# A decode kernel that streams its caches: VectorE's program as a loop over head groups, queries projected as rows, 24 instead of 16 blocks of V turned at the end

## The chip, the cores and the metric

One core of a Trainium2 chip. The metric is the device time of one execution in microseconds (us); lower is better. All runs told here were in the undisturbed ("fast") state. The profile is one execution taken by the hardware profiler; its span is about 1.8 us shorter than the time that the same execution reports.

Names: PE is TensorE, DVE is VectorE, ACT is ScalarE, POOL is GpSimd, SP is SyncE, which issues the big DMAs here. The profile counts 16 DMA engines, and each large transfer has 16 completion events in the trace, taken as one per engine. The *lag* is the time from the first of these 16 events of a transfer to the last; where no transfer is named, it is the last piece of V.

## The reference, cut

```python
# A: one decode step of attention.  Hq=16, Hkv=8, Sk=65536, Dh=256, D=448, all bf16
q = (x @ wq).reshape(1, 1, 16, 256)          # two query heads share one K/V head
p = softmax(q @ k.T / 16)                    # k, v: 8 x 65536 x 256 each
a = (p @ v).reshape(1, 1, 4096) @ wo
# B: layernorm(x), an outer product with w1 and b1, gelu, a sum with w2 and b2: 448 numbers
g = sigmoid((x * gate_w).sum(-1))
out = g * a + (1 - g) * b                    # 448 numbers
```

K and V are 268 MB each. Each byte is used once, so the kernel is a stream of 544 MB from HBM with little work on each piece.

## The kernel before

Each of the eight K/V heads (a "group") is cut into six chunks of 6, 6, 5, 5, 5, 5 steps, a step being 16 blocks of 128 rows; 48 chunks in all. A chunk of K is 6 or 5 MB (6144 or 5120 KB in the profile) and goes into one of two buffers; a chunk of V goes into a third. Per chunk VectorE turns K (5 or 6 transposes of 2.28 us), PE computes scores, ScalarE exponentiates, VectorE turns the probabilities, PE multiplies with V one chunk later, VectorE adds the result to `og`. PE's program is already a hardware loop; VectorE's is written out, all 48 chunks of it.

```python
        def load_k(i):
            n = steps[i] * SB * DH
            if i >= 2:
                sp.wait_ge(s_s, cum[i - 1])            # scores of chunk i-2 done
            sp.dma_start(out=kbuf[i % 2][:, 0:n], in_=kv_src(A_k_cache, i)).then_inc(s_k[i % 2], 16)

        def load_v(i):
            n = steps[i] * SB * DH
            if i >= 1:
                sp.wait_ge(s_pv, i)                    # PV of chunk i-1 done
            sp.dma_start(out=vbuf[:, 0:n], in_=kv_src(A_v_cache, i)).then_inc(s_v, 16)
        # ... (cut)
        def project(e):                                # queries as columns: 128 matmuls of one column
            for c in range(2):
                for h in range(HQ):
                    dst = q_ps[:, c * HQ + h:c * HQ + h + 1]
                    for k in range(KA):
                        e.matmul(dst, lhsT=wqa_v[:, k, h, :, c], rhs=xT[:, k:k + 1],
                                 start=(k == 0), stop=False)
                    # ... one more for the last 64 rows of wq (cut)
        # ... (cut)
        for i in range(total):                         # VectorE, straight-line code
            g, c = divmod(i, PER)
            turns(i)
            if 0 < i < total - 1:
                dve.wait_ge(s_pv, i)
                drain_pv((i - 1) % PER == 0)           # two instructions, 256 columns each
                # ... at a group's end: denominators, s_g (cut)
            # ... turn the probabilities, next queries (cut)
```

The last chunk of V arrives in four pieces, of 48, 16, 12 and 4 blocks. The first 64 blocks are used "upright" (probabilities as weights, V as the moving side, then a drain by VectorE and a turn of the result on PE, the "o-turn"). The last 16 are used "turned": V itself is the weights, two matmuls of two columns a block, and they need no drain.

```python
        edges = [0, (steps[-1] - 2) * SB, (steps[-1] - 1) * SB, steps[-1] * SB - TAIL, steps[-1] * SB]
        # ... (cut)
        pe.wait_ge(s_last[0], 16)
        for s in range(steps[-1] - 2):
            p_v(vlast, pT_t[1], s, False, False)
        # ... (cut)
        pe.wait_ge(s_last[1], 16)
        p_v(vlast, pT_t[1], steps[-1] - 2, False, True).then_inc(pe_sem, 1)
        dve.wait_ge(pe_sem, 3)
        drain_pv(False)
        # ... (cut)
        o_turn(2)
        for j in range(SB):
            if j in (0, SB - TAIL):
                pe.wait_ge(s_last[2 if j == 0 else 3], 16)
            # ... two turned matmuls per block (cut)
```

The softmax here doesn't subtract the row's maximum and nothing guards it: scores larger than these inputs give would overflow.

Of the kernel before, what the change touches and what calls it, by code (L numbers as in the profile page):

```python
# [14 lines left out]
HQ = 16  # L15
HKV = 8
# [13 lines left out]

TAIL = 4
# [4 lines left out]
PE = mybir.EngineType.PE  # L36

# [55 lines left out]
def kernel(  # L93
# [55 lines left out]
    one_b = const.tile([1, 128], BF16, name="one_b")  # L149
# [24 lines left out]
    den = [const.tile([128, PER], FP32, name=f"den{i}") for i in range(2)]  # L174
# [3 lines left out]
    og = const.tile([128, DH], FP32, name="og")  # L178
# [8 lines left out]
    M0, M1, R0, R1, D0, D1, DA_, DB_ = range(8)  # L187
    offsets = {
        M0: [(0, 2)], M1: [(2, 4)], R0: [(0, 1), (2, 3)], R1: [(1, 2), (3, 4)],
# [14 lines left out]
    def critical():  # L204
# [9 lines left out]
        s_pv = nc.alloc_semaphore("s_pv")  # L214
        s_g = nc.alloc_semaphore("s_g")
# [15 lines left out]
        def load_k(i):  # L231
            n = steps[i] * SB * DH
            if i >= 2:
                sp.wait_ge(s_s, cum[i - 1])
            sp.dma_start(out=kbuf[i % 2][:, 0:n], in_=kv_src(A_k_cache, i)).then_inc(s_k[i % 2], 16)

        def load_v(i):
            n = steps[i] * SB * DH
            if i >= 1:
                sp.wait_ge(s_pv, i)  # L240
            sp.dma_start(out=vbuf[:, 0:n], in_=kv_src(A_v_cache, i)).then_inc(s_v, 16)
# [34 lines left out]
        for t, key, val in (  # L276
            (one_b, "one_b", 1.0), (xd, "xd", 0.0), (one_f, "one_f", 1.0), (zero_b, "zero_b", 0.0),
            (pat, "pat", 0.0), (qw, "qw", 0.0), (col_f, "col_f", 1.0), (pv, "pv", 0.0),
        ):
            do("dve", lambda e: e.memset(t[:], val), writes=[key])  # L280
# [11 lines left out]
        def turn_x(e):  # L292
            for k in range(KA + 2):
                if k < KA:
                    src = x_row[:, 0:DA].rearrange("o (p k) -> o p k", k=KA)[:, :, k]
                else:
                    src = xd[:, k - KA, :]
                last = e.matmul(
                    x_ps[:, k:k + 1], lhsT=src, rhs=one_b[:, 0:1], start=(k == 0),
# [25 lines left out]
        for col, sign in ((0, -1.0), (1, 1.0)):  # L325
# [25 lines left out]
            "pe", lambda e: e.matmul(xb_ps, lhsT=one_b[:], rhs=x_row[:], start=True, stop=True),  # L351
# [75 lines left out]
        q_ps = misc[:, 448:448 + 2 * HQ]  # L427
        wqa_v = wqa.rearrange("p k (h d two) -> p k h d two", h=HQ, two=2)
        wqb_v = wqb.rearrange("p (h d two) -> p h d two", h=8, two=2)

        def project(e):
            for c in range(2):
                for h in range(HQ):
                    dst = q_ps[:, c * HQ + h:c * HQ + h + 1]
                    for k in range(KA):
                        e.matmul(
                            dst, lhsT=wqa_v[:, k, h, :, c], rhs=xT[:, k:k + 1],
                            start=(k == 0), stop=False,
                        )
                    x_h = KA + h // 8  # L440
                    last = e.matmul(
                        dst, lhsT=wqb_v[:, h % 8, :, c], rhs=xT[:, x_h:x_h + 1],
                        start=False, stop=True,
                    )
            return last

        do("pe", project, reads=["wqa", "wqb", "xT", "x_ps"], writes=["q_ps", "x_ps"])
        do.need("sp", writes=["wqa", "wqb"])
        load_v(0)
        load_wo(0)  # L450
# [23 lines left out]
        def queries(g, r):  # L474
            h = 2 * g + r
            cols = slice(PAD + 16 * r, PAD + 16 * r + 97, 32)
            return dve.tensor_tensor(
                out=qw[:, :, cols], in0=qr[:, :, h:h + 1].to_broadcast([128, 8, 4]),
# [4 lines left out]
        for r in range(2):  # L483
            do("dve", lambda e: queries(0, r), reads=["qr", "block"], writes=["qw"])
# [7 lines left out]
        for i in range(total - 1):  # L492
            if i + 2 < total:
                load_k(i + 2)
            if i + 1 < total - 1:
                load_v(i + 1)
            if i % PER == 0 and i > 0:
                load_wo(i // PER)
# [3 lines left out]
        sp.wait_ge(s_s, cum[total - 1])  # L502
        edges = [0, (steps[-1] - 2) * SB, (steps[-1] - 1) * SB, steps[-1] * SB - TAIL, steps[-1] * SB]
# [7 lines left out]
        user = [0, 0, 0]  # L511
# [3 lines left out]

        def turns(i):
            kn = kbuf[i % 2][:].bitcast(FP32)
            dve.wait_ge(s_k[i % 2], 16 * (i // 2 + 1))
            for t, (s, b) in enumerate(blocks(i)):
                ins = dve.transpose(  # L520
                    out=kT[b][:].bitcast(FP32), in_=kn[:, s * SB * 128:(s + 1) * SB * 128]
                )
                if user[b]:
                    ins._wait_ge(s_s, user[b])
                ins.then_inc(s_kt, 1)
                user[b] = cum[i] + t + 1

        s_d = nc.alloc_semaphore("s_d")
        done = [0]

        def chain(ins, wait=True):
            if wait and done[0]:
                ins._wait_ge(s_d, done[0])
            done[0] += 1
            ins.then_inc(s_d, 1)

        def drain_pv(first):
            if first:
                chain(dve.tensor_scalar(  # L539
                    out=og[:], in0=pv[:, 0:DH], scalar1=mask[:, M0, 0:1], scalar2=None, op0=ALU.mult  # L540
                ))
            else:
                chain(dve.scalar_tensor_tensor(  # L543
                    out=og[:], in0=pv[:, 0:DH], scalar=mask[:, M0, 0:1], in1=og[:],
                    op0=ALU.mult, op1=ALU.add,
                ))
            chain(dve.scalar_tensor_tensor(  # L547
                out=og[:], in0=pv[:, DH:2 * DH], scalar=mask[:, M1, 0:1], in1=og[:],
                op0=ALU.mult, op1=ALU.add,
            ))  # L550

        def den_rows(g):
            chain(dve.tensor_tensor(out=dmul[:], in0=den[g % 2][:], in1=dmask, op=ALU.mult))
            chain(dve.tensor_reduce(out=dsum[:], in_=dmul[:], axis=AXIS.X, op=ALU.add))

        o_ps = misc[:, 504:512].rearrange("p (c v) -> p c v", v=4)
        do.need("dve", reads=["mask", "bias", "hw2", "h_bc", "qr", "w1T", "b1T"])
        do.need("dve", reads=["block"])
        for i in range(total):
            g, c = divmod(i, PER)  # L560
            turns(i)
            if 0 < i < total - 1:
                dve.wait_ge(s_pv, i)
                drain_pv((i - 1) % PER == 0)
                if c == 0:
                    den_rows(g - 1)
                    ins = dve.tensor_scalar(
                        out=og[:], in0=og[:], scalar1=dsum[:, 0:1], scalar2=None, op0=ALU.add
                    )
                    ins._wait_ge(s_d, done[0])  # L570
                    ins.then_inc(s_g, 1)
            pT = pT_t[1 if i == total - 1 else 0]
            ins = dve.transpose(out=pT[:], in_=p_t[:])  # L573
            ins._wait_ge(s_e, i + 1)
            ins.then_inc(s_pt, 1)
            if c == PER - 1 and g + 1 < HKV:
                for r in range(2):
                    queries(g + 1, r)
            if c == 0 and i > 0:
                dve.wait_ge(s_wo, 16 * g)  # L580
                dve.wait_ge(s_o, g)
                chain(dve.reciprocal(out=rden[:], in_=o_ps[:, 0, 2:4]))
                chain(dve.tensor_scalar(
                    out=rden[:], in0=rden[:], scalar1=gate[:, 0:1], scalar2=None, op0=ALU.mult
                ))
                ins = dve.tensor_tensor(
                    out=oT[:].rearrange("p (c r) -> p c r", r=2), in0=o_ps[:, :, 0:2],
                    in1=rden[:].rearrange("p (o r) -> p o r", o=1).to_broadcast([128, 2, 2]),
                    op=ALU.mult,
                )  # L590
                ins._wait_ge(s_d, done[0])
                ins.then_inc(s_ot, 1)
# [4 lines left out]
        for i in range(total):  # L597
            g, c = divmod(i, PER)
            ins = act.activation(  # L599
                out=p_t[:], in_=sc[:], func=ACT.Exp, scale=scale, accum_out=den[g % 2][:, c:c + 1]  # L600
            )
            ins._wait_ge(s_s, cum[i + 1])
# [44 lines left out]
        def scores(s, b, first, last):  # L647
# [8 lines left out]
            ins.then_inc(s_s, 1)  # L656

        def p_v(vt, pT, s, first, last):
            pT = pT[:].rearrange("p (i b x) -> p i b x", b=4, x=16)
            for k in range(SB // 2):  # L660
# [5 lines left out]
                    stop=last and k >= SB // 2 - 4, tile_position=(0, 32 * a), skip_group_check=True,  # L666
# [3 lines left out]
        def o_turn(width):  # L670
            for cc in range(2):
                ins = pe.matmul(  # L672
                    o_ps[:, cc, 0:width], lhsT=og[:, cc::2],
                    rhs=mask[:, R0:R0 + width, 0], start=(cc == 0), stop=(cc == 1),
                    skip_group_check=True,
                )
# [46 lines left out]
        fin = Order.__new__(Order)  # L723
        fin.__dict__.update(do.__dict__)
        for t, (s, b) in enumerate(blocks(last_i)):
            scores(s, b, t == 0, t == steps[-1] - 1)
        pe.wait_ge(s_pt, 1).then_inc(s_pt, -1)
        pe.wait_ge(s_v, 16).then_inc(s_v, -16)
        for s in range(steps[-2]):
            p_v(vbuf, pT_t[0], s, s == 0, False)  # L730
        dlast = (HKV - 1) % 2
        dve_sem = nc.alloc_semaphore("s_fd")
        pe_sem = nc.alloc_semaphore("s_fp")

        den_rows(HKV - 1)
        dve.wait_ge(s_d, done[0])
        dve.nop().then_inc(dve_sem, 1)
        pe.wait_ge(dve_sem, 1)
# [3 lines left out]
        ).then_inc(pe_sem, 1)  # L742
        pe.wait_ge(s_mp, turn)
        pe.matmul(
            acc[0:1, 0:D], lhsT=col_f[:], rhs=ymix[:], start=False, stop=True, skip_group_check=True,
        ).then_inc(pe_sem, 1)
        ins = dve.reciprocal(out=rden[:], in_=den_ps[:, 0:2])
        ins._wait_ge(pe_sem, 1)
        chain(ins, False)
# [97 lines left out]
```

## Time and profile before

| | before |
|---|---|
| time, median (range) of 3 runs | 1269.69 us (1269.68 to 1269.99) |
| span of the profiled run | 1268.7 us |
| data queue, share of 16 engines | 99.3% |
| last V piece: first and last engine to complete | 1258.60 and 1262.89 us |
| from there to the end | 5.8 us |

First, lines of the page of before: span, busy time by engine, and the DMA queues (packets, MB, share of 16 engines' span).

```profile
span 1268.7 us, 10632 instructions
PE 713.1 (56%) x4364; PEld 278.3 (22%) x4364; DVE 673.9 (53%) x511; ACT 50.1 (4%) x127; POOL 76.7 (6%) x98
q1 hardware_dynamic: 16728, 544.22, 99.3%
q8 instruction: 4, 0.07, 0.0%
q14 instruction: 9, 0.07, 0.0%
```

No compute engine is near full and the data queue is: the kernel is bound by the stream. The two "instruction" queues look like nothing, 0.14 MB of 544.

Next, four windows of 1 us near the end of before: length, busy time (and instructions) of PE, PE's weight loads, DVE, ACT and POOL, then the granted TensorE clock, the DMA share, and GB/s.

```profile
1258.00:1259.00 1.00, 0.95 (x12) 0.39 (x16) 0.00 (x0) 0.00 (x0) 0.00 (x0) 0.52 0.70 279
1259.00:1260.00 1.00, 1.00 (x16) 0.28 (x9) 0.00 (x0) 0.00 (x0) 0.00 (x0) 0.50 0.22 86
1260.00:1261.00 1.00, 1.00 (x16) 0.10 (x8) 0.00 (x0) 0.00 (x0) 0.00 (x0) 0.50 0.08 33
1261.00:1262.00 1.00, 0.90 (x16) 0.11 (x8) 0.00 (x0) 0.00 (x0) 0.00 (x0) 0.77 0.06 27
```

The stream does not stop at once. It trickles out at 33 and 27 GB/s, which is what one engine of 16 moves (434/16 = 27). One engine is late. The 16 completion events of the last piece of before, sorted and counted from the first:

```
first engine 1258.60; then +0.01 +0.04 +0.11 +0.29 +0.33 +0.40 +0.50 +0.51 +0.52 +0.53 +1.05 +1.48 +1.54 +2.01 +4.29
largest lag over time:  2.1 to 2.4 (28 to 617 us), 2.8 (from 623), 3.6 (from 910), 4.4 (from 1186)
8192-byte instruction packets at 49, 322, 332, 381, 617, 850, 905, 1184 us; 16384-byte ones at 19, 26, 1255, 1264 us
```

The events do not say which engine they belong to, so "the late engine" is read from how the sorted lags step up, just after a packet. The last two steps, from 2.62 to 3.57 us at 905 and from 3.46 to 4.44 at 1184, are 0.95 and 0.98; between packets the lag shrinks again a little. Up to 617 us the largest lag is that of another engine, late since the packets of 16384 bytes, so the packets at 49 and 332 do not show in it.

The packets carry no engine's name either, but a count gives it: from 49 to 332, 617, 905 and 1184 us the trace records 123, 130, 132 and 129 instructions of VectorE (its waits included), about as many each time (128.5 on average). So these packets are taken as the fetches of VectorE's code, and the code that one of them brings is called a fetch block below.

Last, the tail of before in order of time (start, duration, engine, line, operation, output<-inputs, count, idle time before and what ended it).

```profile
1258.05 2.73 PE L663 MATMUL pv<-kbuf,pT 128*4 128x512 bf16 x24 [2.09 <-DMA kbuf<-in_A_v_cache_dram]
1261.19 0.72 PE L663 MATMUL pv<-kbuf,pT 128*4 128x512 bf16 x8
1262.03 0.48 DVE L543 SCALAR_TENSOR_TENSOR og<-pv,mask,og 128x256 f32<-128x256 f32 x1 [5.36 <-PE pv L663]
1262.55 0.48 DVE L547 SCALAR_TENSOR_TENSOR og<-pv,mask,og 128x256 f32<-128x256 f32 x1
1263.15 0.63 PE L672 MATMUL misc<-mask,og 128*128 128x2 f32 x4 [1.24 <-DVEq L773]
1263.64 0.97 PE L783 MATMUL misc<-pT,kbuf 128*128 128x2 bf16 x32
1264.64 0.16 DVE L789 TENSOR_TENSOR oT<-misc,rden 128x4 bf16<-128x4 f32 x1 [1.61 <-PE misc L783]
1265.76 0.67 SPq L810 DMA_DIRECT2D out_dram<-res  x1
```

The last data is there at 1262.89, but the o-turn (L672) starts only at 1263.15 and the turned matmuls (L783) stand behind it. They end 1.7 us after the last data. A PE at a granted clock of 0.5 is called cold below.

### The profile page before, as it was taken

How to read it: one execution, taken by the hardware profiler on the slowest of the kernel's cores; microseconds unless marked ns; L12 is line 12 of the kernel's file. 1: busy time of each engine (PE TensorE's matmuls, PEld its weight loads, DVE VectorE, ACT ScalarE, POOL GpSimd, SP SyncE). 2: the span in 40 equal slices, each digit the busy share in tenths (PEclk: the TensorE clock that was granted, in tenths of full speed). 3: DMA queues.
4: the chain of work that ended last, by engine and by line, in shares of the span. 5: the costliest groups of instructions: out<-in, count | busy, mean ns of one | idle time of the engine just before them, and what ended most of it. 6: DMA issues, size and time to landing. Idle time of an engine off the chain costs nothing. (4 is left out here: it accounts for less than half of the span.)

```text
span 1268.7 us, 10632 instructions
## 1 busy us (share of the span) xinstructions
PE 713.1 (56%) x4364; PEld 278.3 (22%) x4364; DVE 673.9 (53%) x511; ACT 50.1 (4%) x127; POOL 76.7 (6%) x98
## 2 busy tenths in 40 slices
PE   2845656466444655566556664565545655466546
PEld 1312222122211222222122221222212221122212
DVE  4745555465545645555456554565446644465444
ACT  0000000000000000000000000000000000000000
POOL 0001010110110101101101011000000000000000
PEclk9887877768877787778877787778777888778777
DMA  9999999999999999999999999999999999999996
GB/s 412 420 441 434 425 435 437 431 434 438 439 426 427 434 435 433 438 428 434 440 436 429 430 434 432 434 438 434 434 427 444 427 430 434 436 430 429 436 433 294
DMA packets 16831, 544.36 MB, mean 429 GB/s; under 512 B 1841, under 2 KB 3891, under 8 KB 4275
## 3 DMA queue, kind: packets, MB, share of 16 engines
q1 hardware_dynamic: 16728, 544.22, 99.3%
q8 instruction: 4, 0.07, 0.0%
q14 instruction: 9, 0.07, 0.0%
q10 hardware_dynamic: 90, 0.01, 0.0%
HBM read 544.22 MB, written 0.00 MB: 429 GB/s over the span
## 5 line engine op out<-in xcount | busy, mean ns | idle before, releaser
L652 PE MATMUL sc<-kT,qw 128*128 128x512 bf16 x2048 | 565.0, 438 | 463.9 <-PEq L648 463.9
L520 DVE STREAM_TRANSPOSE kT<-kbuf 128x2048 f32<-128x2048 f32 x256 | 571.2, 2283 | 328.1 <-DMA kbuf<-in_A_k_cache_dram 292.2
L652 PEld LDWEIGHTS sc<-kT,qw 128*128 128x128 bf16 x2048 | 213.8, 108 | 813.5 <-issue 649.6
L663 PE MATMUL pv<-vbuf,pT 128*4 128x512 bf16 x2008 | 129.2, 409 | 57.2 <-PEq L694 56.8
L573 DVE STREAM_TRANSPOSE pT<-p_t 128x512 bf16<-128x512 bf16 x48 | 34.1, 711 | 95.0 <-ACT p_t L599 95.0
L543 DVE SCALAR_TENSOR_TENSOR og<-pv,mask,og 128x256 f32<-128x256 f32 x39 | 18.9, 483 | 115.3 <-PE pv L663 115.3
L663 PEld LDWEIGHTS pv<-vbuf,pT 128*4 128x4 bf16 x2008 | 50.5, 91 | 133.9 <-issue 93.9
L599 ACT ACTIVATE p_t<-sc 128x512 bf16<-128x512 f32 x48 | 28.7, 597 | 1192.7 <-PE sc L652 1192.7
L626 POOL TENSOR_SCALAR t_b<-t_b 128x448 f32<-128x448 f32 x14 | 7.9, 564 | 358.5 <-ACT t_b L608 358.5
L630 POOL TENSOR_SCALAR t_b<-t_b,hw 128x448 f32<-128x448 f32 x14 | 9.2, 660 | 335.6 <-ACT t_b L616 335.6
L547 DVE SCALAR_TENSOR_TENSOR og<-pv,mask,og 128x256 f32<-128x256 f32 x47 | 22.7, 484 | 1.7
L539 DVE TENSOR_SCALAR og<-pv,mask 128x256 f32<-128x256 f32 x8 | 3.9, 484 | 36.7 <-PE pv L663 36.7
L629 POOL TENSOR_TENSOR t_b<-t_b,u_b 128x448 f32<-128x448 f32 x14 | 15.8, 1127 | 1.2
L634 POOL TENSOR_TENSOR t_b<-t_b,u_b 128x448 f32<-128x448 f32 x14 | 15.8, 1126 | 1.2
L635 POOL TENSOR_TENSOR ymix<-ymix,t_b 128x448 f32<-128x448 f32 x14 | 15.8, 1126 | 1.1
L716 PE MATMUL acc<-wo,oT 128*1 128x448 bf16 x28 | 7.4, 391 | 13.7 <-PEq L713 13.7
L608 ACT ACTIVATE t_b<-h_bc,b1T,w1T 128x448 f32<-128x448 f32 x14 | 10.5, 748 | 0.0
L622 POOL TENSOR_SCALAR u_b<-h_bc,w1T,b1T 128x448 f32<-128x448 f32 x14 | 10.0, 714 | 4.1 <-DVE pat L419 2.7
L599 ACT ACTIVATION_READ_ACCUMULATOR p_t<-sc 128x1 f32 x48 | 9.3, 194 | 0.0
L616 ACT ACTIVATE t_b<-t_b 128x448 f32<-128x448 f32 x14 | 7.9, 566 | 0.0
L672 PEld LDWEIGHTS misc<-mask,og 128*128 128x128 f32 x32 | 4.9, 195 | 2.9 <-DVEq L773 1.9
L716 PEld LDWEIGHTS acc<-wo,oT 128*1 128x1 bf16 x28 | 2.0, 84 | 15.9 <-issue 14.6
(88 smaller groups left out, 60.5 us busy)
## 6 DMA issues: line engine op xcount, KB each, us to landing
kbuf<-in_A_k_cache_dram SPq DMA_DIRECT2D x32, 5120.0 KB, 32.0
vbuf<-in_A_v_cache_dram SPq DMA_DIRECT2D x31, 5120.0 KB, 21.7
kbuf<-in_A_k_cache_dram SPq DMA_DIRECT2D x16, 6144.0 KB, 35.8
vbuf<-in_A_v_cache_dram SPq DMA_DIRECT2D x16, 6144.0 KB, 25.4
wo<-in_A_wo_dram SPq DMA_DIRECT2D x8, 448.0 KB, 23.8
vbuf<-in_A_wq_dram SPq DMA_DIRECT2D x1, 3072.0 KB, 10.0
kbuf<-in_A_v_cache_dram SPq DMA_DIRECT2D x1, 3072.0 KB, 27.1
kbuf<-in_A_v_cache_dram SPq DMA_DIRECT2D x1, 1024.0 KB, 29.1
```

Source lines behind the costliest of these rows:

```text
L520: ins = dve.transpose(out=kT[b][:].bitcast(FP32), in_=kn[:, s * SB * 128:(s + 1) * SB * 128])
L543: chain(dve.scalar_tensor_tensor(out=og[:], in0=pv[:, 0:DH], scalar=mask[:, M0, 0:1], in1=og[:], op0=ALU.mult, op1=ALU.add,))
L547: chain(dve.scalar_tensor_tensor(out=og[:], in0=pv[:, DH:2 * DH], scalar=mask[:, M1, 0:1], in1=og[:], op0=ALU.mult, op1=ALU.add,))
L573: ins = dve.transpose(out=pT[:], in_=p_t[:])
L599: ins = act.activation(out=p_t[:], in_=sc[:], func=ACT.Exp, scale=scale, accum_out=den[g % 2][:, c:c + 1])
L608: ins = act.activation(out=t_b[:], in_=h_bc[:], func=ACT.Square, scale=w1T[:, b:b + 1], bias=b1T[:, b:b + 1],)
L622: lambda: pool.tensor_scalar(out=u_b[:], in0=h_bc[:], scalar1=w1T[:, b:b + 1], scalar2=b1T[:, b:b + 1], op0=ALU.mult, op1=ALU.add,),
L629: lambda: pool.tensor_tensor(out=t_b[:], in0=t_b[:], in1=u_b[:], op=ALU.mult),
L634: lambda: pool.tensor_tensor(out=t_b[:], in0=t_b[:], in1=u_b[:], op=ALU.mult),
L635: lambda: pool.tensor_tensor(out=ymix[:], in0=ymix[:], in1=t_b[:], op=ALU.add),
L652: ins = pe.matmul(sc[:], lhsT=qw[:, q, at:at + 128], rhs=kv[:, :, q // 2, :, q % 2], start=(first and q == 0), stop=(last and q == 7), ski ...
L663: ins = pe.matmul(pv[32 * a:32 * a + 4, :], lhsT=pT[:, k, :, ROW0 + s], rhs=vt[:, j * DH:(j + 2) * DH], start=first and k < 4, stop=last a ...
```

## The change

The intent: less instruction traffic beside the data (VectorE loops over head groups; PE's code ahead of its loop gets shorter), and a shorter tail. The loop needs waits that are the same in every turn, so each wait also takes back what it waited for (`take`), and SP's loads now wait for one counter, `s_vf`, raised when VectorE has drained a chunk; V and the next K are issued together. The drain becomes one instruction over 512 columns. The diff, cut to its core:

```diff
@@ SP: what a load waits for, and the order of the loads
-                sp.wait_ge(s_s, cum[i - 1])
+                sp.wait_ge(s_vf, i - 1)
-                sp.wait_ge(s_pv, i)
+                sp.wait_ge(s_vf, i + 1)
-        for i in range(total - 1):
-            if i + 2 < total:
-                load_k(i + 2)
-            if i + 1 < total - 1:
-                load_v(i + 1)
+        load_k(2)
+        for i in range(1, total - 1):
+            load_v(i)
+            ...
+            if i + 2 < total:
+                load_k(i + 2)
@@ queries projected as rows, then turned
+            for n in range(8):
+                half, a = divmod(n, 4)
+                dst = q_rows[half][32 * a:32 * a + 1, :]
+                for k in range(KA):
+                    e.matmul(
+                        dst, lhsT=xT[:, k:k + 1], rhs=wqa[:, k, n * 512:(n + 1) * 512],
+                        start=(k == 0), stop=False, tile_position=(0, 32 * a),
+                    )
+                ...
+        def turn_q(e, a):                    # 32 matmuls in all
+            for h in (2 * a, 2 * a + 1, 2 * a + 8, 2 * a + 9):
+                ...
@@ VectorE
+        def take(eng, sem, n=1):
+            eng.wait_ge(sem, n).then_inc(sem, -n)
         def drain_pv(first):
+            if first:
+                return dve.tensor_copy(out=og[:], in_=pv[:])
+            return dve.tensor_tensor(out=og[:], in0=pv[:], in1=og[:], op=ALU.add)
-        for i in range(total):
-            g, c = divmod(i, PER)
-            ...
+        dve_chunk(0, None)
+        with nc.Fori(0, HKV - 1, 1, engines=[DVE], head_slot={DVE: 0}) as turn_v:
+            for i in range(1, PER + 1):
+                dve_chunk(i, turn_v * 2 + 2)
+        for i in range(total - PER + 1, total):
+            dve_chunk(i, None)
@@ tail (TURN = 24, TAIL = 4)
-        edges = [0, (steps[-1] - 2) * SB, (steps[-1] - 1) * SB, steps[-1] * SB - TAIL, steps[-1] * SB]
+        edges = [0, nlast - TURN - SB, nlast - TURN, nlast - TAIL, nlast]
```

`head_slot={DVE: 0}` asks for the loop's first instruction at the start of a fetch block. The tail's pieces become 40, 16, 20 and 4 blocks, and the o-turn has four matmuls instead of two, because `og` now has 512 columns.

## The prediction

> **What bounds it now.** The DMA stream. The page has the data queue at 99.3% of 16 engines' span, 544.22 MB at 429 GB/s; PE (56%) and VectorE (53%) fit inside. In the completion events (16 per transfer, one per DMA engine) 5 MB follow 5 MB every 12.08 us, 434 GB/s, from start to end. [...] The queue never runs dry: a V load is issued at least 4.8 us before the previous transfer's first engine is done, a K load over 12 us. Only the ends can give.

> **The end.** The completions of the last V piece run from 1258.60 to 1262.89 us. Fifteen engines are done by 1260.61; one is 2.3 us later. Windows of 1 us show it: from 1258 on 279, 86, 33, 27 GB/s, the last about one engine's share. Its lag over the first engine grows in steps: about 1.0 us after 49 us, then 2.0, 2.8, 3.6, 4.4 after the 8192-byte instruction packets at 332, 617, 905 and 1184 us. That spacing fits VectorE's straight-line code [...]: its fetches delay one data engine by 0.7 to 1.0 us each. [...] Two engines lag 1.5 to 2.0 us since the 16384-byte packets at 18.7 and 26.4 us, which fit PE's preamble.
> The chain of waits then: last data 1262.89, turned matmuls done 1264.62, output issued 1265.76, end 1268.7.

> **What changes.**
> 1. VectorE loop: 97 instructions[...]. No fetch from about 60 us to the end: the worst engine falls from 4.3 us to the next one's 2.0. Worth 2.2 us (1.8 to 2.8), all critical.
> 2. Queries as rows: 128 matmuls become 32 of 512 columns plus 32 turns; PE's preamble loses 64 matmuls with weight loads[...]: perhaps one PE fetch less (0 to 0.5 us). The projection gets slower (up to 7 us, estimated from 0.22 us per 512 columns), but the queue holds work to 55 us: nothing.
> 3. Tail: the upright part ends 24 blocks before the end, not 16, so its drain and o-turn (before: o-turn done 1263.8, 0.9 us after the last data) fall before the last data. After it remains part of 48 turned matmuls (26 ns each), about 0.65 us, against 1.73. Worth 1.1 us, less if the granted clock is 0.5 there (as at 1258 to 1261 before).
> 4. One drain of about 0.75 us (estimate from 0.48 for 256 columns) for two of 0.48; K and V issued together after it: V about 0.7 us later, margin still about 4 us. Nothing.

> Sum: 2.2 + 0.2 + 0.9 = 3.3 us. Predicted 1266.4 us, 8 in 10 between 1265.2 and 1268.4. Faster by over 2%: 0.00; within 2%: 0.99; slower: 0.01.

> **What would show it.** Right: no regular 8192-byte instruction packets; last completions spread over about 2 us; first engine still at 1258.6; 5 MB every 12.08 us; o-turn before the last landing; last landing to end 4.6 to 5.0 us (was 5.8).

> **What would make it wrong.** A fetch at every loop turn (several us slower); PE's fetch after its loop hitting the engine that lags already (+1 us); V issued too late, so the first engine's end moves; a cold PE in the tail.

For step 1, read the loop's 97 instructions against the 123 to 132 that the trace of before records from one VectorE packet to the next. That the steady rate could not rise was not shown; measured is 434 GB/s from start to end. The 0.22 us per 512 columns is the median step of the score matmuls (L652) in before.

## The result, and the profile after

| | before | after |
|---|---|---|
| time, median (range), 4 runs each | 1269.84 us (1269.68 to 1270.55) | 1268.07 us (1267.97 to 1268.24) |
| span of the profiled run | 1268.7 us | 1266.2 us |
| last V piece: first engine | 1258.60 us | 1258.58 us |
| last V piece: last engine | 1262.89 us (4.29 later) | 1261.27 us (2.69 later) |
| last engine to end | 5.82 us | 4.94 us |

The ratio is 0.9985, 95% interval 0.9968 to 1.0002. Ratios here are the mean time of one kernel's fast runs over that of the other's of the same rounds, so not quite the ratio of the medians. By the 2% rule the verdict is "same"; the ranges of the two kernels do not overlap in this set or in a later one (below).

The profiled run of before was one of its longer ones (1270.49), that of after was typical (1267.99). So the spans differ by 2.5 us and the medians by 1.8.

The same lines of the page, of after:

```profile
span 1266.2 us, 10795 instructions
PE 719.7 (57%) x4344; PEld 281.9 (22%) x4344; DVE 665.2 (53%) x473; ACT 50.1 (4%) x127; POOL 76.8 (6%) x98
q1 hardware_dynamic: 16728, 544.22, 99.5%
q8 instruction: 4, 0.07, 0.0%
q14 instruction: 6, 0.05, 0.0%
```

The middle of the run is as it was: DVE still 53%, and 5 MB (5120 KB) every 12.08 us in the completion events. The queue q14 has fewer packets (6, before 9), q8 (4, the ones of 16384 bytes) has as many. Those of q8 are taken as PE's code: v1, whose PE program is shorter by 24 matmuls, has 3. The windows at the end of after:

```profile
1258.00:1259.00 1.00, 0.26 (x8) 0.00 (x0) 0.69 (x1) 0.00 (x0) 0.00 (x0) 1.00 0.67 266
1259.00:1260.00 1.00, 0.95 (x8) 0.95 (x8) 0.00 (x0) 0.00 (x0) 0.00 (x0) 1.00 0.23 94
1260.00:1261.00 1.00, 0.47 (x14) 0.39 (x14) 0.00 (x0) 0.00 (x0) 0.00 (x0) 0.95 0.12 43
1261.00:1262.00 1.00, 1.00 (x42) 1.00 (x39) 0.00 (x0) 0.00 (x0) 0.00 (x0) 0.50 0.00 0
```

The trickle ends one window earlier, and the clock is near 1.0 in the first three windows, where it was 0.5. In the fourth it is 0.5. The tail of after in order of time:

```profile
1255.27 1.25 PE L787 MATMUL pv<-kbuf,pT 128*4 128x512 bf16 x20 [0.26 <-DMA kbuf<-in_A_v_cache_dram]
1257.65 0.61 PE L787 MATMUL pv<-kbuf,pT 128*4 128x512 bf16 x8 [0.83 <-DMA kbuf<-in_A_v_cache_dram]
1258.31 0.69 DVE L562 TENSOR_TENSOR og<-pv,og 128x512 f32<-128x512 f32 x1 [2.59 <-PE pv L787]
1259.05 1.10 PE L701 MATMUL misc<-mask,og 128*128 128x2 f32 x8 [0.80 <-DVE og L562]
1260.69 1.43 PE L798 MATMUL misc<-pT,kbuf 128*128 128x2 bf16 x48 [0.53 <-DMA kbuf<-in_A_v_cache_dram]
1262.15 0.16 DVE L569 TENSOR_TENSOR oT<-misc,rden 128x4 bf16<-128x4 f32 x1 [3.15 <-PE misc L798]
1262.37 0.54 PE L831 MATMUL acc<-wo,oT 128*1 128x112 bf16 x16 [0.26 <-DVE oT L569]
1263.27 0.67 SPq L841 DMA_DIRECT2D out_dram<-res  x1
```

Now the turned matmuls (L798) wait for data and no longer for the o-turn (L701), which is over at 1260.15. The completion events and instruction packets of after:

```
first engine 1258.58; then +0.05 +0.08 +0.15 +0.17 +0.21 +0.23 +0.55 +0.61 +0.68 +0.80 +1.01 +1.48 +1.57 +2.15 +2.69
8192-byte instruction packets at 42, 48, 322, 383, 848, 1198 us; 16384-byte ones at 26, 32, 1254, 1260 us
```

The packets at 322, 381 to 383 and 848 to 850 us are in both kernels, so they are taken as other engines' code. VectorE's are 49, 332, 617, 905, 1184 before and 42, 48, 1198 after: five against three, not five against one. The largest lag of after was 2.2 us just before the packet of 1198 and 2.85 at the next landing.

### The profile page after: what moved, and what is told of

The parts are those of the page before. It is cut to its first block, busy times and chain, and to the rows that moved or that the text cites. A ratio compares the mean times of both kernels' runs of the same rounds, so it can differ in the third digit from the quotient of the medians.

```text
span 1266.2 us, 10795 instructions
## 1 busy us (share of the span) xinstructions
PE 719.7 (57%) x4344; PEld 281.9 (22%) x4344; DVE 665.2 (53%) x473; ACT 50.1 (4%) x127; POOL 76.8 (6%) x98
## 3 DMA queue, kind: packets, MB, share of 16 engines
q1 hardware_dynamic: 16728, 544.22, 99.5%
HBM read 544.22 MB, written 0.00 MB: 430 GB/s over the span
## 5 line engine op out<-in xcount | busy, mean ns | idle before, releaser
L691 PE MATMUL pv<-vbuf,pT 128*4 128x512 bf16 x2008 | 132.4, 417 | 56.7 <-PEq L725 56.7
L562 DVE TENSOR_TENSOR og<-pv,og 128x512 f32<-128x512 f32 x39 | 27.0, 691 | 111.1 <-DVEq L543 108.5
L561 DVE COPY og<-pv 128x512 f32<-128x512 f32 x8 | 5.5, 691 | 38.9 <-DVEq L543 38.9
L701 PEld LDWEIGHTS misc<-mask,og 128*128 128x128 f32 x64 | 8.7, 196 | 2.3 <-DVE og L562 1.3
L701 PE MATMUL misc<-mask,og 128*128 128x2 f32 (+1 forms) x64 | 8.0, 249 | 0.8 <-DVE og L562 0.8
L747 PEld LDWEIGHTS acc<-wo,oT 128*1 128x1 bf16 x28 | 2.2, 91 | 15.4 <-issue 14.5
```

Of the source, the lines that this page charges most:

```text
L562: return dve.tensor_tensor(out=og[:], in0=pv[:], in1=og[:], op=ALU.add)
L691: ins = pe.matmul(pv[32 * a:32 * a + 4, :], lhsT=pT[:, k, :, ROW0 + s], rhs=vt[:, j * DH:(j + 2) * DH], start=first and k < 4, stop=last a ...
L701: ins = pe.matmul(o_ps[:, cc, 0:width if half == 0 else 2], lhsT=og[:, half * DH + cc:(half + 1) * DH:2], rhs=mask[:, m:m + (width if half ...
L747: ins = pe.matmul(acc[0:1, 0:D], lhsT=oT[:, k:k + 1], rhs=wo[:, r, cc, :], start=False, stop=False, skip_group_check=True,)
```

## The experiments

The theory (**fetch**): each instruction packet delays the one DMA engine that carries it; the kernel ends with its slowest DMA engine; and the tail's gain comes on top. In before an 8192-byte packet is recorded with 0.31 us, and the largest lag steps up by 0.95 and 0.98 us; how the one leads to the other, no run here shows. Rivals: it is all the **tail**; or it is the **order** of the loads and the single drain. All kernels gave correct results. Timed medians stand beside the kernel before of the same call. Runs e1 to e4, c1, e5, v3 and v4 were on one chip, e6, e7, v1 and v2 on another.

**e1: VectorE written out again, all else as after.**

```diff
-        with nc.Fori(0, HKV - 1, 1, engines=[DVE], head_slot={DVE: 0}) as turn_v:
+        for turn_v in range(HKV - 1):
```

> The changed kernel with VectorE's loop written out (97 instructions per group, seven times). Fetch theory: straight-line code of 97 slots per 158 us group crosses a 128-instruction block every 209 us, so 8192-byte instruction packets come back at that spacing, about five more between 60 and 1200 us (before, with fewer instructions, had them every 283 us); each costs one DMA engine 0.7 to 1.0 us, so the slowest engine of the last V piece lands 5 to 6 us after the first (changed kernel 2.7, before 4.3), while the first still lands at 1258.6. From the last landing to the end 4.9 us as in the changed kernel. Span 1268.5 to 1269.5, that is 2 to 3 us over the changed kernel. Rival 'it is all the tail' or 'it is the order of the loads and the single drain': span as the changed kernel, 1266.2.

Measured: 1270.55 us (1270.39 to 1270.62; before 1270.16; ratio 1.0003), span 1268.7. VectorE's packets came at 40, 263, 479, 688, 921 and 1128 us, about every 218, with 126 to 130 recorded VectorE instructions from one to the next. The largest lag stepped up by 0.95 to 0.97 us at each of the last three. It ended at 4.72 us (expected 5 to 6). The last landing to the end took 4.93 us. So this one part carries the gain: without the loop the changed kernel is no faster than before. It has six VectorE packets and before has five, since the change's waits make the code longer (789 recorded VectorE instructions against 623). The first engine, too, was 0.5 us later (1259.07). The events show where: the V load issued at 1156.53 had only 1.65 us until the first engine ran dry (after: 4.50), and its transfer took 15.0 us instead of 14.5. A late engine holds back a chunk's completion (a K chunk's last engine at 1136.95 us; after: 1133.80), VectorE turns that chunk later and drains later (at 1155.82), that holds back the next issue, and at the margin the fast engines then idle. There the lag fell from 5.32 to 4.85 us, which is why it missed its forecast. In e4, below, the same load has a margin of 1.42 us and the same 15.0. This chain is read from the two traces and was not tested by itself.

**e2: the kernel before with only the tail's 24 turned blocks.**

```diff
-        edges = [0, (steps[-1] - 2) * SB, (steps[-1] - 1) * SB, steps[-1] * SB - TAIL, steps[-1] * SB]
+        nlast = steps[-1] * SB
+        edges = [0, nlast - TURN - SB, nlast - TURN, nlast - TAIL, nlast]     # TURN = 24
```

> The kernel before with the tail's 24 turned blocks alone. Fetch theory: completions of the last V piece unchanged (slowest 4.3 us after the first, at 1262.9), last landing to end 4.9 to 5.1 us instead of 5.8, so 0.7 to 0.9 us less than before. Rival 'it is all the tail': the whole gain, 1.8 us or more.

Measured: 1269.68 us (1269.58 to 1269.94; before 1270.16; ratio 0.9997). Lag 4.34 us, last landing (the last completion event of all) 1262.88, then 4.91 us to the end. As expected: the landing is untouched and the tail is worth 0.9 us in the profile, 0.5 in the medians. "All the tail" falls.

**e3: the loop's head asked for at slot 64 of a fetch block.**

```diff
-head_slot={DVE: 0}
+head_slot={DVE: 64}
```

> The changed kernel with the loop's first instruction at slot 64 of a fetch block instead of 0, so that the 97 instructions lie across a boundary of 128. Nothing else moves. Fetch theory: [...]each of the seven turns fetches again, one or two 8192-byte packets a turn, 7 to 14 more in all; at 0.8 us each the slowest engine of the last piece lands 8 to 14 us after the first, and the time is 5 to 11 us over the changed kernel. If both halves stay held: no more packets, and the time of the changed kernel within 0.5 us. The rivals have no reason for any difference.

Measured: 1268.05 us (1267.93 to 1268.19; before 1270.16; ratio 0.9984), lag 2.64 us. VectorE's packets: 42, 48 and 168 us, and none at 1198. The packet of 168 comes 120 us after that of 48, inside the loop's first turn, so the loop is taken to cross a block boundary in each of its seven turns; it fetched for it once. So both halves stay held, the second of the two forecasts (the first was a fetch in each turn). And the packet of 1198 moved to 168 without a change in number or in time: here it counted how many new blocks the code enters, not when.

**e4: e1 with 16 turned blocks.**

```diff
 (as e1)
-TURN = 24
+TURN = 16
```

> The changed kernel with VectorE straight-line and only 16 turned blocks: what is left of the change is the new projection, the single drain, and K and V issued together. Fetch theory: as e1 plus 0.7 to 0.9 us at the end (last landing to end 5.6 to 5.9), span 1269.3 to 1270.4, at or over the kernel before. Rival 'order of loads and single drain': still 1.8 us or more under before, the first engine's last landing earlier than 1258.6.

Measured: 1271.01 us (1270.66 to 1271.21; before 1270.16; ratio 1.0007). With the loop and the 24 blocks taken out, nothing of the gain is left: "order and single drain" falls. The rest of the change may even cost time: the median is 0.85 us over before and the ranges just miss each other, though the interval of the ratio (0.9993 to 1.0020) includes 1. There are six VectorE packets instead of five, the lag is 4.61 us, and the first engine is 0.7 us later (1259.33). But the tail missed its forecast: 5.00 us from the last landing to the end, not 5.6 to 5.9, with the same pieces of V as before. Its lines:

```profile
1258.97 1.47 PE L787 MATMUL pv<-kbuf,pT 128*4 128x512 bf16 x24 [0.92 <-DMA kbuf<-in_A_v_cache_dram]
1262.89 1.10 PE L701 MATMUL misc<-mask,og 128*128 128x2 f32 x8 [0.80 <-DVE og L562]
1263.86 0.97 PE L798 MATMUL misc<-pT,kbuf 128*128 128x2 bf16 x32
```

The same 24 upright matmuls took 1.47 us here and 2.73 us before. PE had idled 0.92 us ahead of them instead of 2.09, and its clock was 1.0, not 0.5. What sets the clock, the traces do not show. Here the longer idle time went with the lower clock, but idle time just before does not settle it alone: in after, from 1261 to 1262 us, PE was 100% busy at a clock of 0.5. So part of what I had put down to the 24 blocks was a cold PE.

**e6: the kernel before, PE kept busy ahead of the last V.** Eight filler matmuls whose result nobody reads.

```diff
+        for k in range(8):
+            pe.matmul(
+                sc[:], lhsT=qw[:, k, 0:128], rhs=kT[0][:, 0:512], start=True, stop=True,
+                skip_group_check=True,
+            )
         pe.wait_ge(s_last[0], 16)
```

> The kernel before with eight filler matmuls (result unused) on PE while it waits for the last V piece. Clock theory: in the profile of before PE stood idle 2.1 us, was granted 0.5 of its clock from 1258 to 1261, and the upright part took 2.73 us for 24 matmuls; e4, also with 16 turned blocks, had clock 1.0 there and took 1.47. So with the filler the clock is 1.0, last landing to end 4.9 to 5.1 us instead of 5.8, 0.4 to 0.9 us faster than before, the runs close together. Theory of the prediction (it is the 24 blocks that do it): 5.6 to 5.9 us as before. Completions of the last piece unchanged, 4.3 us apart, in both.

Measured: 1270.01 us (1269.58 to 1270.15; before 1269.82; ratio 0.9999). Lag 4.44 us; 5.38 us from the last landing to the end, between the two forecasts. From its order of time and then its windows:

```profile
1258.21 1.47 PE L663 MATMUL pv<-kbuf,pT 128*4 128x512 bf16 x24
1262.40 1.01 PE L672 MATMUL misc<-mask,og 128*128 128x2 f32 x4 [1.24 <-DVEq L778]
```

```profile
1258.00:1259.00 1.00, 1.00 (x18) 0.40 (x20) 0.00 (x0) 0.00 (x0) 0.00 (x0) 1.00 0.69 274
1262.00:1263.00 1.00, 0.60 (x3) 0.60 (x4) 0.29 (x1) 0.00 (x0) 0.00 (x0) 0.67 0.04 16
```

The upright part ran at a clock of 1.0, as forecast. But the clock was 0.67 from 1262 to 1263 us, and the two o-turn matmuls (four records) took 1.01 us instead of 0.63. The filler, and the clock with it, is worth 0.44 us (5.82 less 5.38) of the profile's 0.88. In the medians the filler did nothing: 0.2 us over before, with ranges that overlap.

**e5: the changed kernel with 16 turned blocks** (`TURN = 16`, nothing else), with the changed kernel again as **c1**.

> The changed kernel again, unedited, so that the others of this call have it on their own chip: 1267.9 to 1268.3, 1.6 to 2.3 us under before, slowest engine 2.7 us after the first, last landing to end 4.9 to 5.0.

> The changed kernel with 16 turned blocks instead of 24, one number changed. e6 and e4 say that a PE at full clock and the single drain already bring the o-turn to just before the last landing, so that 24 adds little on top: last landing to end 5.0 to 5.1 against 4.94, time 0.1 to 0.5 us over the changed kernel. Theory of the prediction (the 24 blocks are worth 0.9 by themselves): 5.6 to 5.9, time 0.7 to 0.9 over.

Measured: c1 1268.05 us (1267.97 to 1268.37; before 1270.28, range 1269.63 to 1270.82; ratio 0.9984), lag 2.89, 4.95 us to the end. e5 1268.55 us (1268.40 to 1269.26; ratio 0.9989), lag 2.96, 5.05 us. So on top of the rest, the 24 blocks are worth 0.1 us in the profiled tails and 0.5 in the medians; e1 against e4 says the same (0.07 and 0.46). Why the medians give more is open: e5's runs spread over 0.9 us, c1's over 0.4, and a PE that is cold in some runs only would do that, but only profiled runs have a trace.

**e7: the changed kernel with the old projection** (`project` as before, its reads and its output restored, nothing else).

> The changed kernel with the queries projected as before, as columns, all else kept. Fetch theory: two 16384-byte PE packets in the first 60 us with either projection, so the slowest engine stays 2.6 to 2.8 us after the first and the span within 0.3 us of 1266.2. What the prediction gave this part: up to 0.5 us slower without it. Rival (the projection as rows is worth something at the start): the first engine's last landing later than 1258.6.

Measured: 1268.17 us (1267.91 to 1268.26; before 1269.82; ratio 0.9985), span 1266.3, lag 2.76. Two 16384-byte packets, at 20 and 26 us, as with the new projection (26 and 32). The projection as rows, in itself, is worth nothing here. (c1, on the other chip, took 1268.05.)

**v1: fewer new blocks.** The loop stays where the code ahead of it ends, and the queries are turned by 8 matmuls, each serving four heads through a strided identity, instead of 32.

```diff
-        with nc.Fori(0, HKV - 1, 1, engines=[DVE], head_slot={DVE: 0}) as turn_v:
+        with nc.Fori(0, HKV - 1, 1, engines=[DVE]) as turn_v:
@@ turn_q
+                        at = c * HQ + 8 * half + hh
+                        last = e.matmul(
+                            q_ps[:, at:at + 7:2],
+                            lhsT=q_row[0:97, half, hh * DH + c:(hh + 1) * DH:2],
+                            rhs=ident[0:97, 0:97:32], start=(half == hh == c == 0),
+                            stop=(half == hh == c == 1), skip_group_check=True,
+                        )
```

> The changed kernel with VectorE's loop left where the code ahead of it ends (no gap up to a block boundary) and the queries turned by 8 matmuls instead of 32. Fetch theory: VectorE enters one fewer new block, so its 8192-byte packets fall from three (42, 48, 1198 us) to two; PE's preamble fits its first block, so one 16384-byte packet less in the first 60 us (one instead of two). The slowest engine of the last V piece is 1.6 to 2.2 us after the first instead of 2.7, span 1265.2 to 1265.8 against 1266.2. If fetches do not matter: span as the changed kernel.

Measured: 1267.25 us (1267.13 to 1267.77; before 1269.82; ratio 0.9980, 0.9966 to 0.9993), span 1265.5, lag 1.91 us. The instruction queues of v1:

```profile
q8 instruction: 3, 0.05, 0.0%
q14 instruction: 5, 0.04, 0.0%
```

One packet less on each queue: VectorE's at 42 and 1183 us, PE's at 26 us alone. Both counts as forecast, and the time went down: 0.9 us under e7, the kernel nearest to after on this chip. The two edits were not run apart. The trace shows the two effects one after the other: the largest lag is 1.5 us until VectorE's packet of 1183 (in after 2.2 until 1198), and 1.77 after it.

**v2: v1 with eight turns of the loop, the last one cut short by a branch.**

```diff
+        with nc.Fori(0, HKV, 1, engines=[DVE]) as turn_v:
+            for i in range(1, PER - 1):
+                dve_chunk(i, None)
+            turns(PER - 1)
+            with dve.If_lt(t_reg, HKV - 1):
+                dve_rest(PER - 1, turn_v * 2 + 2)
+                dve_chunk(PER, None)
+            dve.reg_add(t_reg, t_reg, 1)
+        dve_rest(total - 1, None)
@@ (memsets of one_f, zero_b, pat and col_f: on POOL instead of VectorE)
```

> v1 with VectorE's loop run eight times (the last turn skips its end by a branch), so that the code after the loop is short, and some memsets moved to another engine. Fetch theory: one or no VectorE packet after 40 us and none near 1200 us; the slowest engine is then one that PE's fetches delayed, 1.5 to 2.2 us after the first; span as v1 or up to 0.4 us less. If a branch inside the loop or the moved memsets cost something at the start, it is hidden under the queue: no change there.

Measured: 1267.29 us (1267.01 to 1267.68; ratio 0.9978), lag 1.69. No VectorE packet near 1200. After 40 us there were two short packets that could be its own, at 55 and 275; the latter seems to be POOL's, since the packet at 381 to 383 is gone and POOL has 14 more instructions. No gain over v1: the lag fell by 0.2 us and the first engine was 0.24 later (1258.84), for a reason I don't know.

**v3 and v4: v1 and v2 with the turned piece cut once more.** In after, all 48 turned matmuls wait for the 20-block piece.

```diff
-        edges = [0, nlast - TURN - SB, nlast - TURN, nlast - TAIL, nlast]
+        edges = [0, nlast - TURN - SB, nlast - TURN, nlast - 12, nlast - TAIL, nlast]
@@ and one more wait between the turned matmuls
```

> v1 with the turned part's transfer cut once more (12 and 8 and 4 blocks instead of 20 and 4). In the changed kernel all 48 turned matmuls (1.43 us) start only when the 20-block piece is complete, 0.63 us before the last landing. With the cut, 24 of them run earlier: last landing to end 4.3 to 4.6 us instead of 4.9, everything before it as v1 (last landing near 1260.5), time 0.4 to 0.6 us under v1, that is 1266.6 to 1266.9.

> v2 with the same cut. As v3 within 0.3 us: 1266.5 to 1267.0.

Measured: v3 1266.89 us (1266.70 to 1267.28; before 1270.28; ratio 0.9975), lag 2.01, 4.33 us to the end. v4 1266.63 us (1266.39 to 1267.22; ratio 0.9974, 0.9960 to 0.9987), lag 1.72, 4.34 us. From v4's order of time:

```profile
1259.03 1.66 PE L807 MATMUL misc<-pT,kbuf 128*128 128x2 bf16 x48
1260.72 0.16 DVE L569 TENSOR_TENSOR oT<-misc,rden 128x4 bf16<-128x4 f32 x1 [2.71 <-PE misc L807]
1260.94 0.37 PE L842 MATMUL acc<-wo,oT 128*1 128x112 bf16 x16 [0.25 <-DVE oT L569]
```

The matmuls start 1.2 us before the last landing (1260.27), and VectorE follows 0.45 us after it, against 0.88 in after. That is 0.43 of the 0.60 us by which the end is shorter. The other 0.17 is the output projection (L842), 0.37 us against 0.54 (L831 in after): the clock was 1.0 from 1260 to 1261 us and 0.65 in the next window here, and 0.5 from 1261 on in after. v4 beats both kernels: 3.65 us under before and 1.42 under the changed kernel (c1) on the same chip.

The dose and the response, from the profiled runs; in v1 and v4 another engine may be the slowest:

| kernel | VectorE packets | slowest engine behind the first |
|---|---|---|
| e1, loop written out | 6 | 4.72 us |
| before | 5 | 4.29 us |
| after, c1 | 3 | 2.69, 2.89 us |
| e3, head at slot 64 | 3 | 2.64 us |
| v1 | 2 | 1.91 us |
| v4 | 1 (or 2) | 1.72 us |

From after to before a packet costs 0.8 us of lag. From after to e1 it is 0.7, or 0.8 with the 0.5 us by which the first engine came later. Both are less than the step of 0.95 to 0.98 at the packet, since part of a step is made up later. From before to e1, for one packet more, it is 0.4, or 0.9 with the later first engine.

## Why the prediction was right or wrong

The time, 1268.07 us, lies inside the range and 1.7 over the middle. The mechanism held; the size of the gain did not (3.3 forecast, 1.8 in the medians, 2.5 in the profiles).

- **"The DMA stream" bounds it, "only the ends can give": right.** First engine at 1258.58 (forecast 1258.6), 5 MB every 12.08 us, q1 at 99.5%.
- **Step 1, "No fetch from about 60 us to the end: the worst engine falls to the next one's 2.0. Worth 2.2 us": this is the step that failed in size.** The fetches behind it were real, as e1 shows. But the loop's entry cost two packets (42 and 48 us), and leaving it, where the code after it runs on into a new block, cost one more at 1198. Until 1198 us the largest lag was 2.2, close to the forecast 2.0, and of an engine late since PE's packets at 26 and 32. The packet of 1198 made VectorE's engine the worst again (2.85, at the end 2.69), and the last landing came 1.62 us earlier instead of 2.2. I had counted only the loop's body and not the blocks around it. v1, with one block less on each engine, shows the remainder: 1.91 us.
- **Step 2, "perhaps one PE fetch less (0 to 0.5 us)": nothing.** Two large packets either way (e7). It took v1's 8 turning matmuls to lose one. The projection's own matmuls did not get slower, against the forecast ("up to 7 us"): by the order of time they ran from 12.96 to 16.57 us, before from 12.92 to 16.50. But the rows have to be copied and turned, so the queries (`qT`) were there at 21.6 us instead of 18.8: 2.8 us later, hidden as forecast.
- **Step 3, tail, 0.9: the size was right in the profile (0.88), the reason only in part, so the match is partly luck.** The forecast "about 0.65 us after the last data" measured 0.85, since all 48 matmuls waited for the 20-block piece. And before's 1.73 was inflated by a cold PE: e6 takes back 0.44 by a warm one alone, and with the single drain besides, e4 and e5 have 5.00 and 5.05 with 16 blocks. The 24 blocks by themselves add 0.1 to that in the profiles. I had seen the clock of 0.5 but named it as a risk of the new tail, not as a cost of the old one.
- **Step 4, order of loads and single drain, "nothing": right for the stream** (smallest margin of a V load 4.4 us, forecast about 4, before 4.8; drain 0.69, forecast 0.75). In the tail the single drain does help: 0.74 us from its start to the o-turn in e4, against 1.11 in e6.
- **The base was wrong by 0.8 us.** I took a gain read from a profile of a 1270.49 us run off a median of 1269.69. The profiled run was a long one, and part of what the change removes (the cold tail) may not have been in the median run at all.

Left open: what each part of v1 is worth by itself; why before spreads over 1.2 us (1269.63 to 1270.82) where after spreads over 0.4; and which DMA engine carries which packet, since the events carry no engine.
